# mLSTM cell and squared-ReLU FFN on one Trainium2 core: two more chunks attended in 64x64 quarters, and the first group's FFN2 placed ahead of the third group's FFN1

## The chip, the cores and the metric

The kernel runs on one core of one Trainium2 chip. The metric is device time in microseconds (us), start to end of one execution. PE is the engine for matrix products, DVE the vector engine, ACT the scalar engine, POOL GpSimd, SP the engine whose queue issues most transfers.

## The reference

Inputs are q, k, v and three gates for 4 batches, 8 heads, 768 steps, head width 40, all float32, and two FFN weights that arrive as float64. The first part is a recurrence over the steps, the second an FFN on its 3072 rows of 320:

```python
for t in range(S):
    m_new = np.maximum(f[:, :, t] + m, i[:, :, t])
    fs = np.exp(f[:, :, t] + m - m_new); is_ = np.exp(i[:, :, t] - m_new); m = m_new
    C = fs * C + is_ * outer(v[t], k[t]);  n = fs * n + is_ * k[t]
    y[:, :, t] = sigmoid(o[:, :, t]) * (C @ q[t]) / np.maximum(np.abs(n @ q[t]), 1.0)
h = np.maximum(x @ w_in, 0.0)          # x: y as rows; w_in 320 x 2048
out = h * h @ w_out                    # w_out 2048 x 320
```

## The kernel before

**Chunks.** The 768 steps of a batch are six chunks of 128 (`NB`), so there are 24, counted `s` = 0 to 23; all eight heads of a chunk are done together. A chunk needs: scores (k times q), weights W (exponential of a masked gate sum `A_bc`), `weighted` (their product P), the products of P with v, the carried state C, and the state after it. Chunk s = 5 closes batch 0 and makes no state. Two chunks are a group of FFN rows, `g` = 0 to 11.

**Two ways to attend.** Up to s = 5, `attend` uses full-height products: `hi` (state, L622), `dC` (new state, L634), `hp` (P and v, L645). `normalise` makes the rows x, and `turn_rows` transposes them on PE (L848, L850) with a copy on ACT (L853). From `X_SQ` = 6 on, `attend_begin` and `attend_end` use 64x64 quarters into `numT` (state L708, P and v L727, new state L738). Between the two halves stands a handshake: DVE reads one element of the first half and writes it to a spare place that the second half's operand covers (L700). The result comes out turned, so it goes through 32x32 blocks and memory: `store_num`, `load_num`, `normalise_turned`, `store_rows`, `load_rows`, `turn_squares`. `decays` (ACT) and `scale_q` (DVE, L672) prepare q times the decay. From `KQ_SQ` = 7 on, k and q are turned in the same way: `pair_up`, `load_squares`, `turn_kq`.

**The FFN.** `ffn1` of groups 0 and 1 is four plain parts each. From group 2 on, FFN1 is a seven-product scheme in two halves (`ffn1_open`, `ffn1_close`, with `sums_of_x` on the input and `sums_of_win` on the weights), each product X, Y, V, Z being blocks of four matmuls (L1041) and small rows (L1090). FFN2 of group 0 is plain (`ffn2`, L911: four parts, two row blocks by two halves of `w_out`); later groups use the same scheme (`ffn2_fast`, L965) with weight sums T0, T1, T2 and a changed `w_out` block (`sums_of_weights`), and input sums S1, S2, S4 (`sums`).

**The weights** come as 18 pieces. Each is fetched raw (SP), split into words on ACT (`words`), joined by three DVE instructions (L231, L235, L236) and one POOL addition (L240). `join` also issues the fetch of a later piece, whose buffer the join frees. `NEXT` and `LAST` say how many pieces are joined by which point.

**Order.** There is no planner: each engine carries out its instructions in the order in which the code issues them. A first loop, `u` = 0 to 7, does the FFN1 of groups 0 and 1 with chunks 2 to 5: even `u` makes scores of s = 2 + u // 2 and the next chunk's weights, odd `u` attends. A second loop runs over `parts`, with n = 0, 1, ... and four parts to a chunk (from s = 6): at n % 4 = 1 the chunk is attended, at 2 the next one's weights are made. `parts` begins with FFN1 of group 2 (kind 1) and then FFN2 of group 0 (kind 2).

## Time and profile before

| | us |
|---|---|
| median of 3 runs (lowest, highest) | 491.14 (490.63, 491.87) |
| the profiled execution: time, span | 491.22, 489.4 |
| PE busy, share of the span | 481.7, 98% |
| DVE, ACT, POOL busy | 341.8, 240.4, 215.3 |
| first loop from u = 4 to its end | 57.5 to 89.2 |
| FFN1 of group 2, FFN2 of group 0 | 91.0 to 109.0, 110.0 to 130.0 |
| FFN2 of group 1 begins | 130.8 |

The span is what the profile covers; the rest of the time lies around it. A row of a group gives busy time and the mean of one instruction; an fp32 matmul appears as two records. "Released by" names the instruction that ended an idle time.

### The profile page before, as it was taken

What the parts mean: (1) busy time and instruction counts of PE and PEld (TensorE: products, weight loads), DVE (VectorE), ACT (ScalarE), POOL (GpSimd) and SP (SyncE); (2) the same over time, 40 slices, a digit from 0 to 9 for tenths busy, and PEclk for the clock granted to TensorE, in tenths of its full rate; (3) what the DMA queues carried; (4) which work ended last, traced back from release to release, by engine and by line L of the source; (5) the groups of instructions that cost most, each with busy time, mean ns of one, the idle gap of its engine ahead of it and who ended that gap; (6) DMA issues with size and microseconds to landing.
All of it is one profiled execution on the core that took longest, in us unless ns stands there. A gap on an engine that the chain in (4) does not pass through costs nothing.

```text
span 489.4 us, 15237 instructions
## 1 busy us (share of the span) xinstructions
PE 481.7 (98%) x6169; PEld 449.0 (92%) x6169; DVE 341.8 (70%) x704; ACT 240.4 (49%) x531; POOL 215.3 (44%) x322
## 2 busy tenths in 40 slices
PE   9999999999999999999999999999999999999997
PEld 4886788897799999999999999999999999999996
DVE  7799767888946856957966956857856956635441
ACT  4676996764522650942742941742942640513300
POOL 6455533432679178078179078078174040020000
PEclk9999999999999999999999999999999999999999
DMA  9999997745878579758759778658665612200000
GB/s 185 227 243 227 304 230 183 151 84 140 171 130 199 120 138 225 134 107 212 135 99 219 140 117 208 134 109 213 123 106 129 149 51 82 55 28 2 3 27 29
DMA packets 191096, 68.08 MB, mean 139 GB/s; under 512 B 158833, under 2 KB 180241, under 8 KB 191025
## 3 DMA queue, kind: packets, MB, share of 16 engines
q1 hardware_dynamic: 185280, 57.50, 55.1%
q0 software_dynamic: 5600, 9.50, 8.1%
q8 instruction: 49, 0.80, 0.7%
q14 instruction: 23, 0.18, 0.1%
q10 hardware_dynamic: 144, 0.10, 0.1%
HBM read 54.77 MB, written 18.01 MB: 149 GB/s over the span
## 4 chain that ended last, share of the span: by engine, by line
PE 87%; ACT 5%; SPq 4%; DMA 3%; issue 1%; DVE 0%; ACTq 0%
PE h_ps L965 35%; PE h_ps L1041 26%; PE h_ps L1090 8%; PE h_ps L911 4%; PE h_ps L874 3%; PE numT L727 3%; PE numT L708 2%; DMA lent_t<-in_moe_w_in_dram 1%; PE numT L738 1%; SPq L210 1%; PE tp L575 1%; PE h_ps L575 1%; SPq L1151 1%; ACT g_c L511 1%; DMA raw<-in_moe_w_in_dram 1%; DMA og<-in_o_gate_dram 1%
## 5 line engine op out<-in xcount | busy, mean ns | idle before, releaser
L475 POOL TENSOR_SCALAR_AFFINE_SELECT A_bc<-A_bc 64x512 f32<-64x512 f32 x32 | 22.5, 704 | 80.4 <-ACT kq L492 57.9
L965 PE MATMUL h_ps<-T,S 128*128 128x160 f32 x352 | 51.7, 300 | 0.6 <-ACT g_c L1107 0.6
L1071 ACT COPY r_sb<-h_ps 128x512 f32<-128x512 f32 x18 | 10.5, 585 | 84.2 <-PE h_ps L1041 84.2
L965 PEld LDWEIGHTS h_ps<-T,S 128*128 128x128 f32 x352 | 48.9, 190 | 1.1 <-ACT g_c L1107 0.9
L965 PE MATMUL h_ps<-w_out,g 128*128 128x160 f32 x336 | 49.2, 303 | 0.0
L981 DVE TENSOR_TENSOR y_sb<-y_sb,h_ps 128x160 f32<-128x160 f32 x44 | 14.1, 320 | 47.7 <-PE h_ps L965 47.6
L965 PEld LDWEIGHTS h_ps<-w_out,g 128*128 128x128 f32 x336 | 46.1, 190 | 1.3 <-issue 0.5
L1041 PE MATMUL h_ps<-xT,w_in 128*128 128x128 f32 x320 | 42.8, 278 | 0.0
L1041 PE MATMUL h_ps<-lent_t,w_in 128*128 128x128 f32 x320 | 42.2, 275 | 0.0
L1041 PEld LDWEIGHTS h_ps<-xT,w_in 128*128 128x128 f32 x320 | 38.9, 192 | 1.4 <-issue 1.0
L1090 PE MATMUL h_ps<-xT,w_in 64*64 64x128 f32 x960 | 39.1, 272 | 0.0
L1041 PEld LDWEIGHTS h_ps<-lent_t,w_in 128*128 128x128 f32 x320 | 38.9, 192 | 0.2 <-issue 0.2
L1041 PE MATMUL h_ps<-lent_t 128*128 128x128 f32 x320 | 39.0, 275 | 0.0
L1041 PEld LDWEIGHTS h_ps<-lent_t 128*128 128x128 f32 x320 | 37.3, 192 | 0.0
L505 ACT ACTIVATE A_bc<-A_bc,b_R 128x64 f32<-128x64 f32 (+1 forms) x128 | 35.7, 361 | 1.8 <-POOL A_bc L475 1.4
L1090 PEld LDWEIGHTS h_ps<-xT,w_in 64*64 64x64 f32 x960 | 34.8, 133 | 1.3
L379 POOL DMA_DIRECT2D va<-in_v_dram x56 | 34.2, 619 | 1.8 <-DMA kq_rows<-in_q_dram 1.3
L758 DVE STREAM_TRANSPOSE tn<-numT 128x256 f32<-128x256 f32 x36 | 14.0, 428 | 28.5 <-PE numT L708 19.2
L874 PE MATMUL h_ps<-xT,w_in 128*128 128x256 f32 x128 | 30.1, 385 | 1.6 <-ACT xT L853 1.2
L874 PEld LDWEIGHTS h_ps<-xT,w_in 128*128 128x128 f32 x128 | 23.4, 190 | 6.1 <-POOL w_in L240 1.6
L1033 POOL TENSOR_TENSOR lent_t<-xT 128x128 f32<-128x128 f32 (+1 forms) x18 | 14.6, 833 | 32.7 <-DVE xT L840 32.7
L965 PE MATMUL h_ps<-w_out,g_c 128*128 128x160 f32 x192 | 28.0, 302 | 0.0
(218 smaller groups left out, 1150.0 us busy)
## 6 DMA issues: line engine op xcount, KB each, us to landing
A_bc<-a_slots SPq DMA_DIRECT2D x32, 256.0 KB, 4.4
num_rows<-tn SPq DMA_DIRECT2D x18, 256.0 KB, 2.3
kq<-num_rows SPq DMA_DIRECT2D x72, 64.0 KB, 2.1
raw<-in_moe_w_out_dram SPq DMA_DIRECT2D x7, 640.0 KB, 5.4
kqT<-kq_rows SPq DMA_DIRECT2D x34, 128.0 KB, 3.3
og<-in_o_gate_dram SPq DMA_DIRECT2D x24, 160.0 KB, 4.9
out_dram<-y_sb SPq DMA_DIRECT2D x24, 160.0 KB, 3.1
raw<-in_moe_w_in_dram SPq DMA_DIRECT2D x7, 512.0 KB, 6.9
```

The costliest lines, as they stand in the source:

```text
L379: eng.dma_start(dst[HALVES[n], PR * (1 - late_keys) : PR * (2 - late_keys)], src[HALVES[late_keys], PR * m : PR * (m + 1)],)
L475: nc.gpsimd.affine_select(part, part, compare_op=ALU.is_ge, fill=-1e30, base=0, pattern=[[0, PR], [0, 2], [1, DP]], channel_multiplier=-1,)
L505: nc.scalar.activation(A[0][:, x, to], A[0][:, x, to], AF.Exp, bias=b_R[:, b, c, own, x : x + 1],)
L727: nc.tensor.matmul(d["numT"][m][HALVES[e], i, t0:], lhsT=va_w[s % NKQ][keys, at * D1 : at * D1 + DP], rhs=rhs, start=(s % NB == 0 and i == ...
L758: nc.vector.transpose(to[:, 2 * m : 2 * m + 2], d["numT"][m].rearrange("p c t -> p (c t)"))
L874: nc.tensor.matmul(hs[i][:, n, :], lhsT=w_in[:, a, fb * P : (fb + 1) * P], rhs=xT[:, :, a, :], start=(n == 0 and a == 0), stop=False,)
L911: nc.tensor.matmul(o_ps, lhsT=st["g2", g][:, fb, j * P : (j + 1) * P], rhs=w_out[:, fb, :], start=(fb == 0), stop=(fb == NF - 1),)
L965: nc.tensor.matmul(to, lhsT=lhsT[:, p], rhs=rhs[:, p, :], start=(start and p == 0), stop=(p == NPAIR - 1), skip_group_check=True,)
L981: add = lambda to, a, b: nc.vector.tensor_tensor(to, a, b, op=ALU.add)
L1033: sub = lambda to, a, b: eng.tensor_tensor(to, a, b, op=ALU.subtract)
L1041: nc.tensor.matmul(to[:, n, :], lhsT=lhsT[:, 4 * q + n, :], rhs=rhs, start=(start and n == 0), stop=True, skip_group_check=True,)
L1090: nc.tensor.matmul(to[cols, n, :], lhsT=w_in2[rows, 4 * q + n, cols], rhs=rhs, start=(start and n == 0), stop=True, skip_group_check=True,)
```

## The change

Chunks s = 4 and 5 take the quarters: `X_SQ` goes from 6 to 4. Their masks are laid on W after the exponentials (`mask_W`), since the decays need the unmasked sums; in `u` = 2 the weights and decays of s = 4 are issued ahead of the weight words. They keep the old state's layout (`C_flat`), whose mask `bdm` is replaced by two copies of half height. In the second loop FFN2 of group 0 comes first (its row blocks taken in turn), then FFN1 of group 2, whose special beginning goes. The squares and gates of s = 7 are loaded at `u` = 6, `normalise_turned` of s = 4 and 5 stands at the end of `u` = 7 and in n = 0, `scores(7)` moves to n = 1. The loads of s = 8 and 9 go from SP to POOL and to n = 2 and 3, and their output gates to n = 0, 2 and 3. One piece is joined at n = 0 rather than at `u` = 7, the last at n = 1 rather than n = 4; all four weight sums stand at n = 3 and 4. The diff, without its mechanical parts:

```diff
...
     SQ = 32
-    KQ_SQ, X_SQ, ROT = 7, 6, 8
+    KQ_SQ, X_SQ, ROT = 7, 4, 8
...
         src = src[b, :, c * P : (c + 1) * P, :].rearrange("h p d -> p h d")
-        eng = nc.sync if s < 10 else nc.gpsimd
+        eng = nc.gpsimd
...
         src = src[b, :, c * P : (c + 1) * P, :].rearrange("h p d -> p h d")
-        eng = nc.sync if s < 10 else nc.gpsimd
+        eng = nc.gpsimd
...
+    def mask_W(s):
+        nc.gpsimd.affine_select(
+            st[s]["W"], st[s]["W"], compare_op=ALU.is_ge, fill=0.0, base=0, pattern=[[0, H], [1, P]],
+            channel_multiplier=-1,
+        )
...
         if s % NB > 0:
-            e = st[s]["eA"] = kq_b[2 + s % 2][:, 1].rearrange("p (j two) d -> p j (two d)", two=2)
+            home = kq_b[2 + s % 2 if s >= NB else s - X_SQ - 1]
+            e = st[s]["eA"] = home[:, 1].rearrange("p (j two) d -> p j (two d)", two=2)
...
                 )
-            if s < X_SQ:
+            if s < NB - 1:
...
-    C_old = []
+    C_old, C_flat = [], []
+    def num_tile():
+        return old.tile([P, 4 * P], F32, name="num", bufs=1)
...
             Cd = st[s]["Cd"] = old.tile([P, PR, 2, D1], F32, name="Cd", bufs=1)
+            if s >= X_SQ:
+                st[s]["Cd"] = Cd = Cd[:].rearrange("p j i d -> p (j i d)")[:, : PR * D1].rearrange("p (j d) -> p j d", d=D1)
+                for i, rows in enumerate(HALVES):
+                    nc.gpsimd.tensor_tensor(
+                        Cd[rows], C_old[(s - 1) % 2][rows, :, i, :],
+                        st[s]["dec"][rows, i::2].unsqueeze(2).to_broadcast([DP, PR, D1]), op=ALU.mult,
+                    )
+                return
             nc.gpsimd.tensor_tensor(
-                Cd[:].rearrange("p j i d -> p (j i) d"), C_old[(s - 1) % 2][:].rearrange("p j i d -> p (j i) d"),
+                Cd[:].rearrange("p j i d -> p (j i) d"), C_old[(s - 1) % 2].rearrange("p j i d -> p (j i) d"),
...
             Cn = C_old[s % 2]
-            if c == 0:
-                nc.vector.tensor_tensor(Cn[:], dC[:], bdm[:], op=ALU.mult)
+            for i in range(2 if c == 0 else 0):
+                nc.vector.tensor_copy(Cn[HALVES[i], :, i, :], dC[HALVES[i], :, i, :])
...
     LIVE = [slice(DP * i, DP * i + D) for i in range(2)]
+    def state(s):
+        return (C_b if s >= NB else C_flat)[s % 2]
...
         else:
-            end, spare = out[1][DP : DP + 1, P : P + 1], C_b[(s - 1) % 2][0:1, 4 * D1 : 4 * D1 + 1]
+            end, spare = out[1][DP : DP + 1, P : P + 1], state(s - 1)[0:1, 4 * D1 : 4 * D1 + 1]
...
         d = st[s]
-        C = C_b[(s - 1) % 2]
+        C = state(s - 1)
...
                 i, j = rows[m], 2 * m + e
+                at = (2 * j + i if s == X_SQ else j) * D1
                 nc.tensor.matmul(
-                    d["numT"][m][HALVES[e], i, :], lhsT=C[LIVE[i], j * D1 : j * D1 + DP], rhs=d["eA"][LIVE[i], j, :],
+                    d["numT"][m][HALVES[e], i, :], lhsT=C[LIVE[i], at : at + DP], rhs=d["eA"][LIVE[i], j, :],
...
             values_of_C(s, (1, 0))
-        tn = attn.tile([P, P // SQ, PR, SQ], F32, name="tn", bufs=1)
-        to = tn[:].rearrange("p m c r -> p c m r")
+        if s < NB:
+            tn = num_tile()[:].rearrange("p (m c r) -> p m c r", c=PR, r=SQ)
+        else:
+            tn = attn.tile([P, P // SQ, PR, SQ], F32, name="tn", bufs=1)[:]
+        to = tn.rearrange("p m c r -> p c m r")
...
         if c + 1 < NB:
-            Cn = C_b[s % 2][:, : PR * D1].rearrange("p (m x) -> p m x", m=2)
+            Cn = state(s)[:, : PR * D1].rearrange("p (m x) -> p m x", m=2)
...
     def load_num(s):
-        N = st[s]["N"] = kq_b[s % 2][:, 1].rearrange("p h d -> p (h d)")
+        N = st[s]["N"] = kq_b[s % 2 if s >= NB else s - X_SQ - 1][:, 1].rearrange("p h d -> p (h d)")
...
         if part == 0:
-            st["o_ps"] = ps_h.tile([P, W], F32, name="h_ps")[:, :DM]
-        o_ps = st["o_ps"]
+            st["o_ps", j] = ps_h.tile([P, W], F32, name="h_ps")[:, :DM]
+        o_ps = st["o_ps", j]
...
-    def ffn1_begin(g):
-        new_g2(g)
-        xT = st["xT", g]
-        begun = st["begun"] = [
-            (ps_h.tile([P, 4, P], F32, name="h_ps"), ffn.tile([P, 4, P], F32, name="r_sb", bufs=4)) for _ in range(2)
-        ]
-        for q, (X, m1) in enumerate(begun):
-            blocks(X, F11, xT[:, 0, 0, :], q, True)
-            nc.scalar.copy(m1[:], X[:])
-        for q, (X, m1) in enumerate(begun):
-            blocks(X, F12, xT[:, 0, 1, :], q, False)
     def ffn1_open(g, q):
-        if q == 0 and g > 2:
+        if q == 0:
...
         xT, xs = st["xT", g], st["xs"]
-        begun = st["begun"].pop(0) if g == 2 else None
-        X = begun[0] if begun else ps_h.tile([P, 4, P], F32, name="h_ps")
-        Y, V, Z = [ps_h.tile([P, 4, P], F32, name="h_ps") for _ in range(3)]
+        X, Y, V, Z = [ps_h.tile([P, 4, P], F32, name="h_ps") for _ in range(4)]
         st["f1"] = X, Y, V, Z
-        m1 = begun[1] if begun else ffn.tile([P, 4, P], F32, name="r_sb", bufs=4)
-        U2, U4 = [ffn.tile([P, 4, P], F32, name="r_sb", bufs=4) for _ in range(2)]
+        m1, U2, U4 = [ffn.tile([P, 4, P], F32, name="r_sb", bufs=4) for _ in range(3)]
         st["U"] = U2, U4
-        if not begun:
-            blocks(X, F11, xT[:, 0, 0, :], q, True)
-            nc.scalar.copy(m1[:], X[:])
+        blocks(X, F11, xT[:, 0, 0, :], q, True)
+        nc.scalar.copy(m1[:], X[:])
...
-    NEXT = (5, 8, 10, 11, 12, 13, 14, 16)
+    NEXT = (5, 8, 10, 11, 12, 13, 14, 15)
...
                     idle(3)
-                turn_rows(s - 1)
+                if s - 1 < X_SQ:
+                    turn_rows(s - 1)
...
             if u == 2:
+                weigh(4, masked=True, vw=False)
+                decays(4)
...
             if u == 2:
-                mask(s + 1)
                 rounding.join()
+                mask_W(4)
                 rounding.join()
-                weigh(s + 1, masked=True)
+                values(4)
...
                     relu_half()
-                weigh(s + 1, masked=(u == 0), vw=(u > 0))
+                weigh(s + 1, masked=(u != 6), vw=(u == 6))
+                if u == 4:
+                    mask_W(5)
                 square_half()
+                if u > 0:
+                    scale_q(s)
+                if u == 6:
+                    load_squares(7)
+                    load_A(7)
...
                 half_tanh(3)
-            load_A(s + 2)
+            if u < 7:
+                load_A(s + 2)
...
                     half_tanh(r)
-            attend(s)
+            if s < X_SQ:
+                attend(s)
+            else:
+                attend_begin(s)
+                attend_end(s)
...
                 values(s + 1)
-            normalise(s)
+            if s < X_SQ:
+                normalise(s)
+            else:
+                store_num(s)
...
                 rounding.join()
-            for r in {5: (8,), 7: (9,)}.get(u, ()):
-                load(r)
-            for r in {5: (7,), 7: (8,)}.get(u, ()):
-                pair_up(r)
             if u > 4:
-                load_o(2 * s)
-                load_o(2 * s + 1)
+                pair_up(s + 3)
+                load_num(s)
...
             square_half()
+            if u == 5:
+                decays(5)
+            if u == 7:
+                normalise_turned(4)
+                store_rows(4)
...
         nc.gpsimd.memset(t[:], 0.0)
-    parts = [(1, 2, i) for i in range(4)] + [(2, 0, i) for i in range(4)]
-    for g in range(1, NG):
+    parts = []
+    for g in range(NG):
...
             parts += [(1, g + 2, i) for i in range(4)]
-    LAST = (17, 17, 17, 17, 18)
-    assert LAST[-1] == len(pieces)
+    ROUNDED = (17, 18)
+    assert ROUNDED[-1] == len(pieces)
...
     for n, (which, g, i) in enumerate(parts):
-        s, at = 6 + n // 4, n % 4
-        if n == 5:
+        s, at = NB + n // 4, n % 4
+        if n == len(ROUNDED):
...
             do(mask, s + 1)
-            if n > 4 and not even and not fast:
+            if not even and not fast:
...
             do(decay_C, s + 1)
-            if s > X_SQ and not fast and not even:
+            if not fast and not even:
                 do(turn_squares, s - 1)
-            if even:
+            if even and s > NB:
...
             do(store_num, s)
+            if n == 1:
+                load_rows(5)
+                turn_squares(4)
...
                 do(load_A, s + 2)
-        if 5 <= n < 8:
-            sums_of_weights(n - 5)
-        if n == 6:
-            sums(1, slice(0, NPAIR), (1, 2))
+        if n == 1:
+            sums_of_win(2)
         if n == 8:
-            sums_of_weights(3)
...
             sums(g, slice(0, NPAIR), (3 + i,))
-        if n == 0:
-            ffn1_begin(g)
-            sums_of_x(g)
-            sums_of_win(2)
-        if at == 3 and s >= 8 and s % 2 == 0 and s // 2 - 1 < NG:
+        if at == 3 and even and s // 2 - 1 < NG:
...
                 do(turn_squares, s - 1)
-            if n > 4:
-                do(scale_q, s + 1)
+            do(scale_q, s + 1)
...
                 ffn1_close(g, i // 2, i == 1)
-                if at == 1 and g > 2:
+                if at == 1:
...
         elif g == 0:
-            ffn2(g, *divmod(i, 2))
+            ffn2(g, i % 2, i // 2)
...
             ffn1_square()
-            if n < 4:
-                do(turn_kq, s + 1)
-                do(scale_q, s + 1)
...
                 do(load_A, s + 2)
-            if s > 6:
+            if s > NB:
...
             do(load_rows, s)
-            if s == 6:
-                do(pair_up, s + 3)
-        if s == 7 and at == 2:
-            pair_up(s + 3)
+            if s == NB + 1:
+                pair_up(s + 3)
+        if n in (2, 3):
+            load(6 + n)
+            load_o(8 + n)
...
             do(pair_up, s + 3)
-            do(pair_up, s + 4)
-        if s == 7 and at == 3:
+            if s > NB:
+                do(pair_up, s + 4)
+        if s == NB + 1 and at == 3:
             load(s + 3)
-        if even and at == 3:
+        if even and at == 3 and s > NB:
             do(load, s + 4)
+        for x in {3: (0, 1), 4: (2, 3)}.get(n, ()):
+            sums_of_weights(x)
+        if n in (6, 7):
+            sums(1, slice(0, NPAIR), (n - 5,))
...
             ffn1_square()
-        if n < 5:
-            while rounding.done < LAST[n]:
+        if n < len(ROUNDED):
+            while rounding.done < ROUNDED[n]:
...
```

## The prediction

> **What bounds the kernel now.** I read the page's busy shares and slices first, then busy time by stage, then the waits, then the chain of waits. `s` counts chunks from 0, so "chunks 5 and 6" are s = 4 and 5. Busy shares, and two rows of the 40 slices:
>
> ```profile
> PE 481.7 (98%) x6169; PEld 449.0 (92%) x6169; DVE 341.8 (70%) x704; ACT 240.4 (49%) x531; POOL 215.3 (44%) x322
> PE   9999999999999999999999999999999999999997
> DVE  7799767888946856957966956857856956635441
> ```
>
> PE is busy from first slice to last; DVE is at eight or nine tenths around slices 8 to 11. Busy time in the two stages that the change touches (start:end, length, PE, PEld, DVE, ACT, POOL):
>
> ```profile
> 57.50:91.00 33.50, 32.34 (x237) 26.61 (x235) 23.37 (x38) 28.45 (x57) 13.15 (x9) 1.00 0.95 201
> 91.00:130.90 39.90, 39.62 (x515) 33.06 (x513) 33.85 (x66) 23.90 (x52) 16.69 (x25) 1.00 0.61 125
> ```
>
> PE lacks 1.2 us in the first and 0.3 in the second; DVE has only 6 us free of 39.9 in the second. The waits (who, for whom: total, count, longest):
>
> ```profile
> ACT mag L220 <- DMA raw<-in_moe_w_in_dram: 4.6, 2, 4.3
> PE h_ps L874 <- ACT xT L853: 1.2, 1, 1.2
> PE numT L738 <- DVE kq L700: 0.3, 1, 0.3
> ```
>
> The second is PE's idle time at 60.56: ACT came late with a copy because it stood 4.27 us (44.6 to 48.9) for a raw weight piece. The third is the handshake of a chunk in quarters: PE's second half waits for a one-element DVE instruction that reads the first half's end. From the chain of waits (start, length):
>
> ```profile
> 65.35 1.05 PE hi L622 x8
> 66.40 0.89 PE dC L634 x8
> 67.29 1.75 PE hp L645 x16
> ...
> 74.47 0.37 PE tp L848 x2
> 74.83 0.37 PE tp L850 x4
> ...
> 81.01 1.05 PE hi L622 x8
> 82.06 1.75 PE hp L645 x16
> ...
> 114.54 0.38 PE numT L708 x8
> 114.92 0.44 PE numT L727 x16
> 115.36 0.26 PE numT L738 x16
> 115.85 0.44 PE numT L738 x16
> 116.29 0.46 PE numT L727 x16
> 116.97 13.12 PE h_ps L911 x48
> ```
>
> From 60.56 to 485.90 the chain is nearly all PE, so any PE time saved or lost before 131 us moves the end one for one, if no other engine becomes late.
>
> **What the skill says.** "TensorE: Matmul & The Clock Gate", Part 3, The mechanism: matmuls on separate tiles of the array overlap. The trace agrees: s = 7 in quarters lasts 2.43 us (114.54 to 116.97), s = 4 in full tiles 3.70. The same page, Architectural detail: "ACT/DVE are strict FIFO", and, in What's actually happening, an idle window of about 3.4 us halves PE's clock. Here PE's granted clock stays in the top tenth in all slices; its longest wait is 1.2 us, so no run shows the drop. "SBUF — State Buffer", Who interferes with whom: a DVE instruction with two SBUF inputs contends with a GpSimd instruction that reads SBUF. This agrees in kind: the multiply at L672 took 1.23 us at 124.90, beside POOL's multiply at 124.27, and 0.69 at 107.09 with no POOL work.
>
> **Gains, on PE's path.**
> 1. `weigh(4)` and the new `decays(4)` go ahead of the weight words on ACT: 2.6 + 1.25 us inside ACT's 4.27 us wait. The words still start at 48.9, but the eight exponentials no longer follow them, so `xT` is copied about 1.3 us earlier. PE's wait goes: -1.16, and -0.24 where the product at 52.65 ran 3.79 us against 3.55. `mask_W` takes the mask's place on POOL; POOL was idle 1.62 us there.
> 2. s = 4 in quarters: 3.70 to 2.43, -1.27 (handshake included).
> 3. s = 5 has no state to make: 2.80 to 0.38 + 0.44 + 0.28 (handshake) + 0.33 + 0.4 = 1.8, -1.0.
> 4. No `turn_rows(4)` and `(5)`: 2 x 0.74, -1.47.
>
> Sum -5.2: `scores(6)` would end at 85.9, not 91.06.
>
> **At nothing.** The FFN work of group 2 and FFN2 of group 0 keep their PE counts. Three memsets (0.37 + 0.23 + 0.23) leave POOL ahead of 6.2 us and one (0.38) comes at 16.7, and chunk 0's state is two DVE copies (2 x 0.33) for one multiply (0.49); the next PE work that reads it, at 17.86, follows PE's own products without a wait. Chunks 4 and 5 on DVE: normalising in rows (5.0 + 3.6) against quarters (multiply 0.69, handshake 0.16, two transposes 0.78, rows 1.84, turn 0.53, each twice, and 0.35) is +0.1 in all. ACT drops two copies of 0.48 and a small exponential, and adds four of 0.62 and two of 0.47: covered, ACT has 5 us free before 91, but at s = 5's load of gates it runs 1 us later.
> SP: each new round trip issues a store (0.34), four reads (1.75), a store of rows (0.38) and four reads (1.85), 4.3 us, about what the loads of s = 8 and 9 took (0.42 + 1.28 + 2.57). `load_squares(7)` and `load_A(7)` go in ahead of them at u = 6 (3.41 and 0.41 to issue), 10 us before they are read. The two loads go to POOL after `values(7)`, 7 issues each, 0.79 + 1.24 + 2.45 = 4.5; queued behind them are `mask(8)` and the decayed state, wanted by ACT at 122: two loads end near 116, so they hide with 4 us to spare. Without that cover `weigh(8)` slips.
>
> **Losses: DVE's queue.** Group 2's FFN1 used to be PE's cover while DVE worked; now FFN2 of group 0 is. Each stall below is PE waiting for DVE, with times after the gain.
> a. Between `scores(6)` and the handshake of s = 6, DVE has `weighted` 1.2, `turn_kq(7)` 1.16, one piece's words 1.87, `normalise_turned(5)` 1.84, another piece 1.87, handshake 0.2: 8.1 us, to 94.0. PE has FFN2 4.5, the first half 0.7, `scores(7)` 0.88: 6.1 us, to 92.0. **Stall 2.0.** Behind the handshake wait the rest of s = 6 and all of PE.
> b. `weigh(7)` now stands on ACT behind the copy of FFN2's first output, so it begins when part n = 2 ends: copy 0.42, eight exponentials 2.33, `weighted(7)` 1.2, `normalise_turned(6)` 1.84, three of four input sums 0.9: 6.7. PE has one part 4.37 and four blocks 0.9: 5.3. **Stall 1.4** before the second product of group 2.
> c. Four weight sums (1.45 + 1.42 + 1.42 + 1.42) were spread over four parts; two now stand ahead of group 2's first two evacuating additions and two behind them: 7.2 us with two additions of 0.6 and the last input sum, to the handshake of s = 7. PE has three products 2.7, first half 1.0, rows 1.77: 5.5. **Stall 1.8.**
> d. From there to the second product of FFN2 of group 1 (before: 133.12) DVE waits 1.05 for the second half of s = 7, then transposes and state 1.0, waits 0.85 for a product, four additions 2.4, `turn_kq` 1.16, rows 0.48, two additions 1.2, `scale_q` 0.61, `normalise_turned(7)` 1.84, S1 1.2, four additions 2.4, S2 1.2: 15.4. PE has second half 1.05, ten blocks 9.13, rows 1.9, scores 0.7, product 2.28: 15.0. **Stall 0.5.**
>
> Sum +5.7; before's own gaps in that stretch (0.28 and short issue gaps) are not lost a second time: about -0.5. The stalls are nowhere in the trace of before, so both ends: below, none forms (DVE reaches these points 2 us earlier than I place it), 0; above, one in five of some thirty two-input DVE instructions is longer by 0.54, as L672 was, +3. I take the middle, the sum of uncontended rows.
>
> **Sum.** -5.2 + 5.7 - 0.5 = 0.0 on the profiled execution's 491.22 us (span 489.4, 1.8 around it), which stands 0.08 above the median of the runs shown: **491.1**. A difference of 0.3% (1.5 us) is about what can be told from no change.
>
> **Rivals.**
> - *No change: gain and stalls cancel.* As summed, 491.1; own range 489.7 to 492.6. For it: DVE's 85% in the second stage. Against: two sums near 5 us must agree. Chance 0.35.
> - *Faster: DVE keeps up.* If stalls a and c do not form (they rest on DVE's place in its queue within 2 us), 491.1 - 3.8 = 487.3; all gone, 485.4. For it: DVE's total work to group 1's sums grows only by some 3 us. Half the stalls gone gives 488.3. Chance 0.31.
> - *Slower: the reads of s = 5's rows land late.* DVE reaches `normalise_turned(5)` at 90.1. SP frees at 82.3 (it waits for the last raw weight's buffer), stores, issues four gathers (2.5) and the reads (1.75), landing 2.1 later, at 88.9: 1.2 us to spare. From there each microsecond late stops DVE, the handshake of s = 6 and PE alike. The queues are at 0.95 share just before 91; if both trips take the 4.9 us of an output-gate load, not 2.3 and 2.1, the end is 5.4 - 1.2 = 4.2 later, 495.3; half of it, or the contention above, 493 to 494. Chance 0.34.
> - *The change doesn't bring FFN2 forward.* The last `w_out` piece is on DVE until about 99.2 and on POOL (1.54) until 100.8; its columns are wanted near 102.4. 1.6 us late or more, PE just waits in FFN2: 492 to 494, counted under slower.
>
> **Range.** 487.5 to 494.3 leaves out the cases where nearly all stalls vanish or both trips are slow. Chances 0.31 faster, 0.35 same, 0.34 slower.
>
> **What would show it.** Right: no PE idle near 59 us; `scores(6)` ending near 86; PE idle 1.5 to 2.5 us ahead of the second half of s = 6 and of s = 7, released by the one-element DVE instruction; about 1.4 us ahead of group 2's second product, released by DVE's input sums; FFN2 of group 1 starting near 130.5. Wrong: PE idle released by a DMA or POOL (rivals three, four), or FFN2 of group 1 starting before 128.

## The result, and the profile after

| | before | changed kernel |
|---|---|---|
| median of the runs (lowest, highest) | 491.50 of 4 (490.63, 492.04) | 504.49 of 4 (502.65, 506.10) |
| profiled execution: time, span | 491.22, 489.4 | 506.10, 504.4 |
| `scores(6)` ends | 91.06 | 87.39 |
| FFN2 of group 1 begins | 130.84 | 141.77 |
| from there to the end of the span | 358.56 | 362.63 |

The changed kernel is slower: ratio 1.0265, 95% interval 1.0222 to 1.0308. Its profiled execution is the slowest of the four. Line numbers have moved: the handshake is L718, P and v L746, the new state L757, FFN2 of group 0 L933, the FFN1 blocks L1063, FFN2 of later groups L987.

Page of the changed kernel, busy shares and two rows of slices; slices 8 to 11 are now PE's worst, and its granted clock dips there and once later:

```profile
PE 483.6 (96%) x6229; PEld 449.7 (89%) x6229; DVE 340.0 (67%) x719; ACT 242.8 (48%) x534; POOL 225.5 (45%) x335
...
PE   8999999597899999999999999998999999999997
...
PEclk9999999889899999999999999999899999999999
```

and the clock row of the kernel before:

```profile
PEclk9999999999999999999999999999999999999999
```

Busy time by stage (start:end, length, PE, PEld, DVE, ACT, POOL, granted PE clock, DMA share, GB/s):

```profile
57.50:91.00 33.50, 31.62 (x310) 25.27 (x307) 22.46 (x44) 30.44 (x59) 14.30 (x11) 1.00 0.97 218
91.00:110.00 19.00, 13.43 (x128) 9.44 (x127) 10.58 (x25) 2.58 (x4) 6.53 (x7) 0.82 0.59 121
110.00:131.00 21.00, 16.04 (x209) 13.51 (x208) 12.70 (x26) 6.54 (x20) 13.50 (x18) 0.93 0.60 137
```

PE is idle for 10.5 of the 40 us after 91, and in that stretch its granted clock falls, which it did nowhere in the kernel before. DVE is not fuller: 23.3 us where it had 33.9. It waits, too. The waits of the changed kernel (total, count, longest):

```profile
PE numT L757 <- DVE kq L718: 8.1, 3, 5.6
PE h_ps L1063 <- ACT kq L496: 2.7, 1, 2.7
PE numT L727 <- issue: 1.6, 1, 1.6
PE h_ps L896 <- ACT xT L875: 1.0, 1, 1.0
DVE dm L812 <- DMA kq<-num_rows: 8.8, 6, 3.5
```

The first holds 5.57 us at the handshake of s = 6 and 2.27 at that of s = 7. The second is the wait before group 2's second product (2.69); ACT's instruction ended in the same quarter of a microsecond as DVE's input sums, and e2 and e4 below, where the same wait is put down to `lent_t`, show that the sums are what PE waits for:

```profile
119.41 2.02 PE L1063 MATMUL h_ps<-lent_t 128*128 128x128 f32 x16 [2.69 <-ACT kq L496]
...
127.42 0.44 PE L757 MATMUL numT<-vw,kq 64*64 64x41 f32 x16 [2.27 <-DVE kq L718]
```

Where the longest began, in the chain of waits (start, length):

```profile
93.19 2.05 DMA kq<-num_rows
...
97.50 0.41 DVE mag L227
...
99.32 0.17 DVE kq L718
...
99.53 0.67 PE numT L757 x16
...
101.09 10.45 PE h_ps L933 x32
```

and SP's issues (start, length):

```profile
82.66 1.36 SPq L206 DMA_DIRECT2D raw<-in_moe_w_out_dram  x2
84.07 0.46 SPq L795 DMA_DIRECT2D num_rows<-num  x1
...
91.75 1.87 SPq L800 DMA_DIRECT2D kq<-num_rows  x4
```

The store of s = 5's result goes out behind two raw weight pieces of 640 KB; 7.7 us later it has landed and SP can issue the reads. DVE stands 3.53 us for them, then normalises, joins a weight piece and only then does the handshake.

**Where the 15.0 us of span went.** Ahead of `scores(6)` 3.67 gained. From there to FFN2 of group 1, 54.38 us instead of 39.78: waits of 5.57, 2.69 and 2.27, and slow matmuls behind them. From the second half of s = 6 to the end of FFN2 of group 0 it is 16.14 us (99.53 to 115.67); in e2, with no wait there, 13.80. Behind the wait at s = 7, 4.53 us (127.42 to 131.95) against 2.94 in e2. So the clock cost 2.3 + 1.6 = 3.9. After FFN2 of group 1 begins, 4.07 more: a wait of 0.61 before its second product, one of 1.56 at 350.7 for which the trace names nothing, slow matmuls behind that (10.76 us of blocks for 9.13), and rests.

### The profile page after: what moved, and what is told of

It reads as the page before. It is cut to its first block, busy times and chain, and to the rows that moved or that the text cites. A ratio compares the mean times of both kernels' runs of the same rounds, so it can differ in the third digit from the quotient of the medians.

```text
span 504.4 us, 15397 instructions
## 1 busy us (share of the span) xinstructions
PE 483.6 (96%) x6229; PEld 449.7 (89%) x6229; DVE 340.0 (67%) x719; ACT 242.8 (48%) x534; POOL 225.5 (45%) x335
## 4 chain that ended last, share of the span: by engine, by line
PE 82%; ACT 5%; DMA 4%; SPq 4%; DVE 3%; issue 2%; POOL 0%; DVEq 0%; ACTq 0%; POOLq 0%
PE h_ps L987 34%; PE h_ps L1063 25%; PE h_ps L1096 7%; PE numT L746 3%; PE h_ps L933 3%; PE h_ps L896 3%; PE numT L727 2%; PE numT L757 2%; DMA raw<-in_moe_w_out_dram 1%; DMA lent_t<-in_moe_w_in_dram 1%; SPq L206 1%; PE h_ps L579 1%; SPq L1156 1%; PE tp L579 1%; DMA og<-in_o_gate_dram 1%
## 5 line engine op out<-in xcount | busy, mean ns | idle before, releaser
L478 POOL TENSOR_SCALAR_AFFINE_SELECT A_bc<-A_bc 64x512 f32<-64x512 f32 x32 | 24.3, 758 | 83.5 <-ACT kq L496 60.7
L1077 ACT COPY r_sb<-h_ps 128x512 f32<-128x512 f32 x20 | 11.7, 585 | 88.4 <-PE h_ps L1063 88.4
L987 PE MATMUL h_ps<-T,S 128*128 128x160 f32 x352 | 51.7, 300 | 0.6 <-ACT y_sb L1007 0.6
L987 PEld LDWEIGHTS h_ps<-T,S 128*128 128x128 f32 x352 | 48.9, 190 | 1.2 <-ACT y_sb L1007 0.8
L987 PE MATMUL h_ps<-w_out,g 128*128 128x160 f32 x336 | 49.3, 303 | 0.3 <-issue 0.3
L987 PEld LDWEIGHTS h_ps<-w_out,g 128*128 128x128 f32 x336 | 46.1, 190 | 1.7 <-issue 1.1
L1063 PE MATMUL h_ps<-xT,w_in 128*128 128x128 f32 x320 | 44.6, 283 | 0.0
L1063 PE MATMUL h_ps<-lent_t,w_in 128*128 128x128 f32 x320 | 43.7, 281 | 0.0
L1063 PEld LDWEIGHTS h_ps<-xT,w_in 128*128 128x128 f32 x320 | 40.1, 195 | 1.9 <-issue 1.6
L1063 PE MATMUL h_ps<-lent_t 128*128 128x128 f32 x320 | 39.1, 275 | 2.7 <-ACT kq L496 2.7
L1063 PEld LDWEIGHTS h_ps<-lent_t,w_in 128*128 128x128 f32 x320 | 40.5, 198 | 0.0
L375 POOL DMA_DIRECT2D va<-in_v_dram x64 | 39.2, 625 | 2.1 <-DMA kq_rows<-in_k_dram 1.5
L1063 PEld LDWEIGHTS h_ps<-lent_t 128*128 128x128 f32 x320 | 37.3, 192 | 2.8 <-ACT kq L496 2.8
L896 PEld LDWEIGHTS h_ps<-xT,w_in 128*128 128x128 f32 x128 | 23.4, 190 | 6.1 <-POOL w_in L236 1.8
L987 PE MATMUL h_ps<-w_out,g_c 128*128 128x160 f32 x192 | 28.0, 302 | 0.0
```

The costliest lines, as they stand in the source:

```text
L375: eng.dma_start(dst[HALVES[n], PR * (1 - late_keys) : PR * (2 - late_keys)], src[HALVES[late_keys], PR * m : PR * (m + 1)],)
L478: nc.gpsimd.affine_select(part, part, compare_op=ALU.is_ge, fill=-1e30, base=0, pattern=[[0, PR], [0, 2], [1, DP]], channel_multiplier=-1,)
L896: nc.tensor.matmul(hs[i][:, n, :], lhsT=w_in[:, a, fb * P : (fb + 1) * P], rhs=xT[:, :, a, :], start=(n == 0 and a == 0), stop=False,)
L987: nc.tensor.matmul(to, lhsT=lhsT[:, p], rhs=rhs[:, p, :], start=(start and p == 0), stop=(p == NPAIR - 1), skip_group_check=True,)
L1063: nc.tensor.matmul(to[:, n, :], lhsT=lhsT[:, 4 * q + n, :], rhs=rhs, start=(start and n == 0), stop=True, skip_group_check=True,)
```

## The experiments

All times are medians; a ratio is to the kernel before on the same chip, with its 95% interval. The marks and lines are those of one profiled execution each, which can lie off its median: the changed kernel's is the slowest of its four, e12's (493.11) the fastest of its six. Four marks (start of FFN2 of group 0; second product of FFN2 of group 1; first FFN1 product of group 4; from there to the end):

| kernel | FFN2 g0 | g1, second | FFN1 g4 | rest | median | ratio |
|---|---|---|---|---|---|---|
| before | 109.97 | 133.12 | 148.77 | 340.6 | 491.50 | 1 |
| changed | 87.72 | 144.81 | 160.97 | 343.4 | 504.49 | 1.0265 |
| e1 store first | 88.55 | 143.78 | 160.49 | 342.0 | 503.17 | 1.0225 (1.019 to 1.0259) |
| e2 handshake first | 89.98 | 143.69 | 161.02 | 340.8 | 501.14 | 1.0199 (1.0162 to 1.0236) |
| e3 PE kept busy | 86.93 | 140.18 | 155.90 | 340.2 | 498.06 | 1.0135 (1.011 to 1.0161) |
| e4 group 2's side | 90.23 | 141.85 | 157.57 | 340.6 | 498.71 | 1.0144 (1.0114 to 1.0173) |
| e5 order alone | 90.23 | 139.24 | 154.96 | 340.4 | 497.99 | 1.0121 (1.0092 to 1.015) |
| e6 four edits | 86.96 | 142.87 | 158.68 | 341.8 | 502.99 | 1.0221 (1.019 to 1.0252) |
| e7 requeued | 86.42 | 138.04 | 157.93 | 344.4 | 502.25 | 1.0187 (1.0124 to 1.0249) |
| e9 transfers too | 88.16 | 131.81 | 154.96 | 342.3 | 498.86 | 1.0136 (1.0103 to 1.0168) |
| e12 sums on POOL | 87.03 | 132.51 | 150.22 | 341.2 | 496.35 | 1.0102 (1.0074 to 1.0129) |

### e1: the store ahead of the raw pieces

```diff
+            if s >= X_SQ:
+                store_num(s)
+            if u == 7:
+                rounding.hold = False
+                rounding.fetch()
             if u != 3:
                 rounding.join()
...
-            else:
-                store_num(s)
```

`hold` keeps back the fetch of the join at u = 6, so that both raw pieces go out behind the store.

> One edit to the changed kernel: the store of s = 5's turned rows is issued ahead of the two raw weight fetches (640 KB each) that stood in front of it on SP; nothing else moves. Theory A (the transfers: the store and the four reads behind it were late because 1.3 MB of raw weights filled the DMA engines first): the store lands about 2.5 to 3 us after its issue at 82.7 instead of 7.7 us, DVE's wait of 3.53 us for kq<-num_rows before normalise_turned(5) shrinks to under 1, the PE wait at the handshake of s = 6 goes from 5.57 to about 2, the granted clock stays above 0.95 between 91 and 110, and the time is 497.5 to 500 (5 to 7 us below the changed kernel: 3.5 of the wait and 2 to 3 of slow clock behind it). Rival B (the DVE queue alone, or four gathers that are slow whatever stands before them): the handshake wait stays above 4.5 us and the time within 1.5 us of the changed kernel's 504.5.

SP, DVE and PE of e1 (start, length; in brackets the idle time before and who ended it):

```profile
82.67 0.34 SPq L796 DMA_DIRECT2D num_rows<-num  x1
...
93.73 0.65 DVE L813 TENSOR_SCALAR dm<-kq 128x8 f32<-128x8 f32 x1 [1.06 <-DMA kq<-num_rows]
...
98.18 0.66 PE L758 MATMUL numT<-vw,kq 64*64 64x41 f32 x16 [3.38 <-DVE kq L719]
...
99.67 15.08 PE L934 MATMUL h_ps<-w_out,g 128*128 128x320 f32 x48
```

The store landed after 2.2 us instead of 7.6, and DVE's wait fell from 3.53 to 1.06, so the raw pieces in front were most of the delay: theory A's mechanism stands. The four reads, now behind the raw pieces, took 4.2 us (median) instead of 2.0. The theory's time does not stand: PE still waited 3.38 where about 2 was expected, the clock still fell, FFN2 was as slow as before, and 1.3 us is all that the median moved, less than the intervals of the two ratios can tell apart.

### e2: the handshake ahead of normalise_turned(5)

```diff
         if n == 0:
...
-            normalise_turned(5)
-            store_rows(5)
...
             do(attend_begin, s)
+            if n == 1:
+                rounding.step(); rounding.step()
...
+                normalise_turned(5); store_rows(5)
                 load_rows(5)
```

> One edit to the changed kernel: normalise_turned(5) with its store of rows, and the second of the two weight pieces joined in n = 0, go behind the handshake of s = 6 on DVE; the transfers stay as they are. Theory A+ (PE waits because the handshake stands in DVE's queue behind work that waits for a transfer): PE's wait at the second half of s = 6 falls from 5.57 to under 1 us although normalise_turned(5) still waits for its reads until about 95, the granted clock stays at 0.97 or more from 91 to 110, and the time is 495 to 498. If PE instead stops in FFN2 for the last two weight pieces (they are then joined after 94 and wanted near 100), 1 to 3 us of that come back: 497 to 500. Rival B' (the stall only moves on, to the state of s = 6 or to the first sums of group 2, and the clock falls there): 502 or more.

PE and DVE of e2:

```profile
96.06 0.39 PE L757 MATMUL numT<-vw,kq 64*64 64x41 f32 x16
...
96.84 13.19 PE L933 MATMUL h_ps<-w_out,g 128*128 128x320 f32 x48
...
110.67 0.58 DVE L862 STREAM_TRANSPOSE xT<-xT 128x384 f32<-128x384 f32 x1 [3.99 <-DMA xT<-x_rows]
...
116.66 3.46 PE L1063 MATMUL h_ps<-lent_t 128*128 128x128 f32 x16 [5.75 <-DVE lent_t L1058]
```

The wait at s = 6 is gone and FFN2's three parts take 13.19, not 14.81. But PE then waits 5.75 for the input sums: the rows of s = 5 are stored at 105 and read back by 110.6, and all of DVE's work for s = 7 stands behind their turn. The wait moved, as rival B' had it, though 501.14 us lies between its 502 and theory A+'s 500.

### e3: PE kept busy during the wait

```diff
                 do(lambda s: scores(s, ("h", "h")), s + 1)
+            if n == 1:
+                idle(22)
```

> One edit to the changed kernel: 22 matmuls of zeros (128 x 512, bfloat16, to a spare tile) between scores(7) and the second half of s = 6, so that PE is busy during most of its wait there; DVE's wait and the time of the handshake stay as they are (99.3). Theory C (part of the loss is the clock that falls after the idle time): the granted clock stays at 0.97 or more from 91 to 110, the three parts of FFN2 behind it take 13.1 to 13.4 instead of 14.8 and the second half of s = 6 about 0.5 less, and the time is 501.5 to 502.8, some 2 to 3 us below the changed kernel. Rival (the clock fell for another reason, such as the load of the engines over a longer time): the clock is 0.82 to 0.9 there all the same and the time is 504 to 505.5.

PE of e3:

```profile
93.34 4.76 PE L1145 MATMUL idle<-zeros 128*128 128x512 bf16 x21 [0.16 <-issue]
...
98.75 0.44 PE L757 MATMUL numT<-vw,kq 64*64 64x41 f32 x16 [0.65 <-DVE kq L718]
...
99.58 13.19 PE L933 MATMUL h_ps<-w_out,g 128*128 128x320 f32 x48
...
116.36 2.76 PE L1063 MATMUL h_ps<-lent_t 128*128 128x128 f32 x16 [2.69 <-ACT kq L496]
...
124.37 0.44 PE L757 MATMUL numT<-vw,kq 64*64 64x41 f32 x16 [0.72 <-DVE kq L718]
```

The handshake comes as late as before, 11.8 us after FFN2 begins, and the matmuls behind it run at full clock: 13.86 us to the end of FFN2 instead of 16.14. That 2.3 us is shown to be the clock. The median fell by more, 6.4 us: in this execution the wait of 1.56 near 350 and the slow stretch behind it are absent too (rest 340.2, not 343.4), and so is PE's wait near 60. Whether by chance or by where the work lies in time, the runs don't tell. The same holds for the second product of group 2: behind a wait of 2.69 us in both, the two groups of matmuls that follow take 2.76 + 1.91 us here and 2.02 + 1.06 in the changed kernel. These slow matmuls in turn fill most of the wait at s = 7, 0.72 instead of 2.27, and full clock follows it.

### e4: group 2's side

```diff
+            if n == 2:
+                weigh(7, masked=True)
             ffn2(g, i % 2, i // 2)
...
-        for x in {3: (0, 1), 4: (2, 3)}.get(n, ()):
+        for x in {2: (0, 1, 2), 5: (3,)}.get(n, ()):
```

> Two edits to the changed kernel, both behind FFN2 of group 0: the exponentials of s = 7 are issued ahead of the copy of FFN2's first output on ACT, and three of the four weight sums are made at n = 2, where DVE is idle for 7.5 us, the fourth at n = 5. Theory D (PE waits for the two queues): the waits of 2.69 us (second product of group 2) and of 2.27 us (handshake of s = 7) go to under 0.5 each, the slow blocks after the second one (2.07 and 1.60 us instead of 1.06) go with it, the 5.57 us wait at s = 6 stays, and the time is 498 to 500. Rival (one of the two is limited by something else, such as the slowed clock at 110 to 131 or the read of s = 6's rows): a wait of over 1.5 us stays in 117 to 131 and the time is above 501.

PE of e4:

```profile
119.11 2.02 PE L1063 MATMUL h_ps<-lent_t 128*128 128x128 f32 x16 [0.53 <-DVE lent_t L1058]
...
124.65 0.39 PE L757 MATMUL numT<-vw,kq 64*64 64x41 f32 x16
```

The wait of 2.69 is 0.53, that of 2.27 is gone, blocks run at 1.16 and 1.06 behind it, and 498.71 is in the band of theory D: the two queues together were the cause of both; which edit removed which wait was not tried apart. Two shorter waits come later, 0.80 at 133.9 and 0.99 before the second product of FFN2 of group 1.

### e5: the order alone

`X_SQ` is 6 again, with full tiles and `turn_rows` for s = 4 and 5; the rest as changed. In it the query of s = 5 is overwritten by the squares of s = 7 before the state product reads it, so that chunk's values differ; PE's instructions and their order do not.

> One part of the change alone: FFN2 of group 0 ahead of FFN1 of group 2, with its weight sums, late piece and loads where the change has them, but s = 4 and 5 attended in full tiles with turn_rows as before (no quarters, no round trip through memory for them). Theory E (the order costs, through the DVE and ACT queues; the quarters only add the late reads): the wait at the handshake of s = 6 is under 1 us, since neither the wait for kq<-num_rows nor normalise_turned(5) stands before it; the waits before the second product of group 2 (2 to 3 us) and at the handshake of s = 7 (1.5 to 2.5) stay, with 1.5 to 3.4 us of slow clock behind them; the time is 496.5 to 500, that is 5 to 8 over the kernel before. Rival F (the order costs nothing by itself, the quarters' transfers are the whole loss): 490.5 to 493.

PE of e5:

```profile
97.85 0.44 PE L757 MATMUL numT<-vw,kq 64*64 64x41 f32 x16 [1.34 <-DVE kq L718]
...
115.43 3.42 PE L1063 MATMUL h_ps<-lent_t 128*128 128x128 f32 x16 [2.67 <-ACT kq L496]
...
123.44 0.44 PE L757 MATMUL numT<-vw,kq 64*64 64x41 f32 x16 [0.89 <-DVE kq L718]
```

That product takes 3.42 us, not 1.95. With no quarters and no round trip for s = 4 and 5 the time is 5.6 us over before, of the changed kernel's 13.0. Theory E holds in the main: the order costs by itself, and the reads came late only with the quarters' round trip. Two of its waits are not of the size expected: 1.34 at s = 6, where under 1 was, and 0.89 at s = 7, where 1.5 to 2.5 was; the slow product ahead of the latter fills part of it, as in e3. What the quarters win is 3.4 us of PE (1.16 and 0.72 in the attending parts and 1.47 in `turn_rows`, below).

### e6, e7, e9, e12: taking the waits away one after the other

e6 is e1, e2 and e4 together. e7 has e1's store and e4's exponentials, the sum 3 of `w_in` at n = 1, the input sums ahead of `weighted(7)` and `normalise_turned(6)`, and DVE's queue in another order:

```diff
-    WIN_SUMS = {5: 0, 6: 1, 7: 3}
+    WIN_SUMS = {5: 0, 6: 1}
...
             do(attend_begin, s)
+            if n == 1:
+                normalise_turned(5); store_rows(5); load_rows(5)
+                rounding.step(); rounding.step()
...
+            if n == 2:
+                sums_of_x(2)
...
+        for x in {3: (0,), 5: (1,), 8: (3, 2)}.get(n, ()):
```

e9 adds SP's and POOL's queues (`load_rows(6)` behind s = 7's store and reads, `load` of 8 and 9 at n = 3 and 6); e12 adds `sums_of_weights` 0 to 2 on POOL at n = 2 and 5, and the reads of s = 9's squares ahead of those rows.

> The edits of the three earlier runs together: the store ahead of the raw fetches, normalise_turned(5) behind the handshake of s = 6 and behind both weight pieces, the exponentials of s = 7 ahead of FFN2's first copy, the weight sums at n = 2 and n = 5. Theory A+D: the wait at the handshake of s = 6 is under 1 us and the granted clock from 91 to 110 at 0.97 or more. But normalise_turned(5), and so the reads of its rows, come late, and turn_squares(5) stands ahead of all of DVE's work for s = 7 and of the input sums, so PE still waits 3 to 6 us before the second product of group 2, with up to 1.7 us of half clock behind it; no wait at s = 7. Time 494 to 498. Rival (the exponentials of s = 7 were what made that wait): under 1 us there, time 489 to 492.

> The change with DVE's queue put in another order: the store of s = 5 ahead of the raw fetches; the last sum of w_in (1.22 us) from u = 7 to n = 1; the handshake of s = 6 ahead of normalise_turned(5), which keeps its place ahead of the last two weight pieces and has its rows stored and read at once; the exponentials of s = 7 ahead of FFN2's first copy; the input sums of group 2 ahead of weighted(7) and normalise_turned(6); the weight sums at n = 3, 5, 8 and 8. Theory (waits of PE for DVE's queue, and the clock behind each, are the whole loss): no PE wait above 0.7 us between 88 and 131, granted clock 0.97 or more there, FFN2 of group 1 begins 39.5 to 41 us after scores(6) ends (changed kernel: 54.4), and the time is 488 to 491.5, no slower than before by more than 0.3%. Rival (DVE has not the time: about 85% busy before, it is late somewhere else whatever its order): a new wait of 2 us or more, at s = 7 or in FFN2 of group 1, and 493 or more.

> The kernel of e7 with SP's and POOL's transfers put in another order as well: the rows of s = 6 are read back only after s = 7's store and four reads have been issued (in e7 SP stood 5.6 us waiting for those rows to be stored, and s = 7's store, ready at 115, was issued at 122.8), turn_squares(6) goes to n = 10, and the loads of s = 8 and 9 go to n = 3 and 6 instead of 2 and 3. Theory (the 8.4 us wait in FFN2 of group 1 in e7 is this queue of transfers, no want of DVE time): s = 7's store is issued before 118, DVE's wait of 7.3 us for kq<-num_rows at 124 goes to under 1.5, the wait in FFN2 of group 1 to under 1.5, and the time is 488 to 493, level with the kernel before or up to 0.6% from it. Rival (DVE's time is short): the wait stays above 4 us, 497 or more.

> The kernel of e9 with 4.9 us taken off DVE: the weight sums T0, T1 and T2 are made on POOL, at n = 2 and n = 5, where it has no work for s = 7 and 8 pending (about 3 us each there, by its 1.54 us for 640 words), and the reads of s = 9's squares go ahead of the rows of s = 6 on SP. Theory H (after the reorderings DVE's time itself is what holds PE: in e9 PE waits 1.1, 1.0 and 3.8 us in FFN2 of group 1 for DVE, and behind them the clock is halved for 3.4 us): the 3.8 us wait at s = 8's handshake goes to under 1 us and the other two to under 1 together, the second half of s = 8 runs near 136 instead of 141, and the time is 489 to 492.5, level with the kernel before. Rival I (the transfers hold it: DVE waited 2.1 us for kqT<-kq_rows ahead of that handshake): 1.5 us or more stay there and the time is 494 or more. Rival J (POOL's sums slow the DVE instructions beside them by more than they take off): as rival I, with two-input DVE instructions of 128 x 512 at 1.2 instead of 0.68 us between 106 and 125.

PE of e6:

```profile
118.56 3.61 PE L1064 MATMUL h_ps<-lent_t 128*128 128x128 f32 x16 [10.67 <-DVE lent_t L1059]
```

The wait before the second product is 10.67 us, where I expected 3 to 6: the weight sums, now ahead of the input sums, add 4.5 to the late rows. In e7 PE runs without a wait over 0.5 us from 88 to 121, then waits 1.07 for DVE, and FFN2 of group 1 begins at 127.2, 41 us after `scores(6)`, about as the theory had it. Its time does not come out, since then follows (SP, DVE, PE of e7):

```profile
122.82 0.53 SPq L796 DMA_DIRECT2D num_rows<-tn  x1
...
131.35 0.17 DVE L813 TENSOR_SCALAR dm<-kq 128x8 f32<-128x8 f32 x1 [7.34 <-DMA kq<-num_rows]
...
138.04 4.34 PE L988 MATMUL h_ps<-T,S 128*128 128x160 f32 x15 [8.37 <-ACT g_c L1124]
```

s = 7's result was ready at 115; its store went out at 122.8, because SP stood 5.6 us for the store of s = 6's rows, which took 6.1 us beside POOL's loads, against 2.1 in the changed kernel. The Trainium skill, "DMA: Bandwidth & Descriptors", Issuing engines are not separate DMA queues, says that transfers of SP and POOL interleave on the same engines; this trace agrees. In e9 that wait is 1.1 us, but three together (1.1, 1.0, 3.8) and a halved clock behind the last come in FFN2 of group 1 (PE of e9):

```profile
131.81 2.41 PE L988 MATMUL h_ps<-T,S 128*128 128x160 f32 x16 [1.14 <-ACT g_c L1124]
...
141.12 0.66 PE L758 MATMUL numT<-vw,kq 64*64 64x41 f32 x16 [3.76 <-DVE kq L719]
```

In e12 the 3.8 is 0.7 and the 1.0 is gone, but the 1.1 has grown to 3.33 (DVE and PE of e12):

```profile
125.70 0.17 DVE L813 TENSOR_SCALAR dm<-kq 128x8 f32<-128x8 f32 x1 [2.01 <-DMA kq<-num_rows]
...
131.08 1.22 DVE L983 TENSOR_TENSOR S<-S,g 128x1024 f32<-128x1024 f32 x1
...
132.51 2.41 PE L988 MATMUL h_ps<-T,S 128*128 128x160 f32 x16 [3.33 <-ACT g_c L1124]
```

S2, the sum at 131.08, is an operand of the product that waits. The last FFN1 product ends at 124.2; the rows, scores and the first product of FFN2 give PE 5 us. DVE has in that time `normalise_turned(7)` 1.9, S1 1.2, four additions 2.4, S2 1.2, 6.7 us, and starts when the reads of s = 7 land. Of the 3.33 us, 2.01 is DVE's wait for these reads. What is left, 1.3 by subtraction, and 1.14 in e9, where DVE did not wait for them, lies in the order itself: in the kernel before, FFN2 of group 0, some 17.7 us of PE that asks nothing of DVE, lay just there. Theory H's waits came out partly (3.8 to 0.7, not the other two together), and its time did not: 496.35. Two of the six executions of e12 kept full clock throughout (a mean of 1.000) and took 493.11 and 493.85; the other four, at 0.992 to 0.997, took 496.2 to 498.4. No version tried is faster than the kernel before; the best is 1.0102 (1.0074 to 1.0129).

### e8, e10: PE kept busy near 60 us

Five matmuls of zeros at u = 4, added to e7 and to e9.

> The kernel of e7 with five matmuls of zeros (about 1.1 us) between scores(4) and the FFN1 part at u = 4, where PE waits about 1.2 us for the copy of xT. Theory C (a wait of that length can send the clock to half for some 3.4 us, as in two of the four runs so far, where the 16 matmuls behind it took 5.41 us instead of 3.72): these 16 matmuls take 3.72 us and the time is 0.5 to 1.7 us below e7, with less spread. Rival (the halving there comes from something else): no difference beyond 0.5 us.

> The kernel of e9 with the five matmuls of zeros at u = 4 as in e8. Theory C (PE's wait of about 1.2 us for xT at u = 4 halves the clock in some executions): the spread of the times is smaller and the median 0 to 1.5 us below e9. Rival: no difference beyond 0.5 us.

500.49 (498.05 to 503.69) beside e7's 502.25 (498.94 to 504.68), 498.16 beside 498.86: not told apart. In e7's profiled execution the wait at u = 4 was not there to be filled.

### e11: the weight words first again at u = 2

```diff
             if u == 2:
+                rounding.words()
                 weigh(4, masked=True, vw=False)
                 decays(4)
-                rounding.words()
```

> One part of the change undone: at u = 2 the weight words go ahead of the exponentials and decays of s = 4 on ACT again, all else as in the changed kernel. Theory G (ACT waits for the second raw piece until about 52.5 whatever stands before it; the exponentials, once hidden in one wait, now hide in the wait before it, and the decays are new work): 3.9 us of exponentials and decays now stand between the first piece's words, done at 50.1, and the second's, so these begin at 54 instead of 52.5, and PE's wait for xT near 60 goes from 1.0 to about 2.5; the time is 1.5 us above the changed kernel, to 3.2 where the clock drops. Rival (my prediction's reading: the exponentials on ACT decide, and putting them first brings 1.3 us): the wait grows by 1.3 as well, but the second piece's words begin as soon as the exponentials end and a wait for the raw piece never shows, in either order.

ACT at the words of the second piece, in the changed kernel:

```profile
52.53 0.80 ACT L216 ACTIVATE mag<-raw 128x640 f32<-128x640 f32 x1 [2.39 <-DMA raw<-in_moe_w_out_dram]
```

and in e11:

```profile
53.93 0.78 ACT L216 ACTIVATE mag<-raw 128x640 f32<-128x640 f32 x1
```

In e11 the second piece has landed by the time the exponentials are done, and `xT` is copied at 62.15 instead of 60.02; FFN2 of group 0 begins 2.3 us later; 506.86, ratio 1.0315 (1.0254 to 1.0377). Theory G holds for ACT. PE's wait came in another place than I had said: 1.85 us for POOL's `w_in` at u = 3, ahead of the point where it would have waited for `xT`, and half clock behind it (a group of matmuls that takes 3.29 us in the changed kernel took 4.97). The reordering is worth about 2 us beside the other order (the intervals of the two ratios overlap), but it only pays for the decays that the quarters add.

## Why the prediction was wrong

It said 491.1 us, range 487.5 to 494.3, no change the likeliest; 504.49 was measured, above the range. The step that failed is the sum of losses: loss a was sized at 2.0 us and measured 5.57, because the store of s = 5's result was priced as if nothing stood in front of it, and what a wait does to the clock behind it, 3.9 us, was put at nothing. The gain fell short as well. Of the 15.0 us of span, 1.5 is missing gain, 5.3 the losses a to c beyond their sizes, 3.9 the clock and 3.6 the end, loss d taken off; 0.7 is rests. By its steps:

- **Gain 1 did not come (1.40 predicted; u = 4's FFN part began 0.05 later than before).** What failed in it: "the eight exponentials no longer follow" the words. ACT could not use the time: the next words wait for their own raw piece until 52.53. In the kernel before these words also began at 52.52; the exponentials had filled that second wait exactly, so it did not show. Where the piece landed sooner (words at 51.66 in e3) PE's wait was gone. PE and ACT of the kernel before, and PE of the changed one:

```profile
60.56 3.72 PE L874 MATMUL h_ps<-xT,w_in 128*128 128x256 f32 x16 [1.16 <-ACT xT L853]
52.52 0.77 ACT L220 ACTIVATE mag<-raw 128x640 f32<-128x640 f32 x1
60.61 3.72 PE L896 MATMUL h_ps<-xT,w_in 128*128 128x256 f32 x16 [1.01 <-ACT xT L875]
```

- **Gains 2 to 4 came**: the attending parts went from 3.59 to 2.43 and from 2.70 to 1.98, two `turn_rows` (1.47) away; -3.67 in all at `scores(6)`, with nothing from gain 1, against -5.2.
- **Loss a: 2.0 predicted, 5.57.** By subtraction DVE's queue gave the 2.0 (5.57 less DVE's 3.53 wait); the 3.53 is the rival *Slower: the reads of s = 5's rows land late*, mechanism and place as written, with 4.2 for both trips slow. I had written that SP stands until 82.3 for the last raw weight's buffer, and yet priced the store that follows at its usual 2.3 us instead of behind 1.3 MB.
- **Loss b: 1.4 predicted, 2.69**: my chain from the copy to the input sums left out POOL's `vw` (0.75), and PE's part behind the copy took 4.1, not 4.37. **Loss c: 1.8, 2.27**: one weight sum took 1.95. **Loss d: 0.5, 0.61**, near its size; the kernel before has no wait there (the product of the kernel before, then of the changed one):

```profile
133.12 2.34 PE L965 MATMUL h_ps<-T,S 128*128 128x160 f32 x16
144.81 2.41 PE L987 MATMUL h_ps<-T,S 128*128 128x160 f32 x16 [0.61 <-ACT y_sb L1007]
```

  That c came so near its size is in part luck: 0.72 and 0.89 stand in its place in e3 and e5, where the clock fell earlier.
- **The clock: not priced at all, 3.9 us there and about 1.6 near 350.** I quoted the skill's idle window and wrote that no run showed the drop; then I summed three waits of 1.4 to 2 us as if each cost only itself. e3 shows that the matmuls behind the wait at s = 6 are slower because of it; for the stretches behind s = 7 and near 350 it is inferred, not tried.
- **The end: 4.07 us** after FFN2 of group 1 begins, of which only loss d was in a step. 1.56 of it is a wait that the trace gives to nothing. It stands at the same instruction, or its neighbour, between 341 and 355 us, in the changed kernel (1.56) and in e1, e2, e6, e7, e9 and e11 (0.7 to 1.6), is 0.2 to 0.4 in e4 and e12, and absent in before, e3, e5, e8 and e10. Such nameless waits stand in two more places, none in before: in FFN2 of group 1 (0.28 in the changed kernel at 150.7, 0.83 to 0.88 in e1, e11 and e12) and in FFN1 of group 4 (0.7 to 1.67 in e6, e7, e9 and e10). What they are stays open.
- **The signs that I named.** No PE idle near 59: wrong, 1.01 us. `scores(6)` near 86: 87.39. FFN2 of group 1 near 130.5: 141.77. PE idle ahead of the second halves of s = 6 and s = 7 by the one-element instruction: right, though 5.57 at s = 6 is far over the 1.5 to 2.5. Before group 2's second product, by the input sums: right. "PE idle released by a DMA" as the sign of the slower rival: it came at one remove, DVE waiting for the DMA and PE for DVE. That FFN2 lacked its last weight piece did not happen.

Two sums of the prediction are out by 0.1, which changes nothing: the gains add up to 5.1, not 5.2, and loss c's terms give 1.7, not 1.8. My two sums near 5 us did not cancel: the gain was counted whole, the losses without what follows a wait. The rival for *faster*, that DVE keeps up, fails for a reason that the sum of DVE's work hides: DVE was less busy than before, and late because of what stood in front of it.

## What to carry to other kernels

A stage that asks nothing of the other engines is cover for what follows it; moving it forward uncovers the place that it left, and taking the waits away there one at a time shows the next one (s = 6, group 2's sums, s = 7's round trip, FFN2 of group 1), so price the whole stretch with every queue, DMA included, before counting a gain. A PE wait can cost more than itself: the shortest with half clock behind it was 1.16 us (e2), the most that followed was 2.9 us of extra matmul time (e7, 138.04 to 144.16: 6.12 us for what took 3.26 in the changed kernel). Before moving work into a wait, look what the engine waits for next: a second wait that is just filled does not show.

## What the runs showed of the hardware

- PE's clock halved, in some executions, behind a wait of 1.16 us: in e2 behind PE's wait at 60, the same 16 matmuls that took 3.72 us in before and in the changed kernel (waits 1.16 and 1.01) took 5.41, and in e4 behind 1.17 as well:

```profile
61.19 5.41 PE L896 MATMUL h_ps<-xT,w_in 128*128 128x256 f32 x16 [1.16 <-ACT xT L875]
```

  Two stretches of 2 us of e2 (third column from the end: granted clock):

```profile
60.00:62.00 2.00, 0.84 (x5) 0.70 (x4) 1.87 (x4) 2.00 (x7) 0.00 (x0) 0.91 0.89 105
62.00:64.00 2.00, 2.00 (x7) 1.53 (x6) 1.75 (x4) 2.00 (x7) 0.46 (x1) 0.50 1.34 178
```

  The Trainium skill, "TensorE: Matmul & The Clock Gate", What's actually happening, has PE at half clock after an idle window of about 3.4 us, and a free-running window of 3413 ns, from which it would follow that it matters where in it a wait falls. The length agrees: 1.69 us lost at half clock are 3.4 us of it, and the longer stretches are multiples. Behind the 5.57 us wait of the changed kernel the granted clock in stretches of 2 us from 96 on is 0.88, 0.50, 0.50, 0.50 and 0.92, together 6.8 us of half clock, of which some 4.8 fall behind the end of the wait; half of that is the 2.3 us lost, within 0.1. In e7 the half clock lasts 10.2 us. The coming and going between executions agrees too. That the array must idle for a whole window does not: a wait of 1.16 us was enough, though narrow transposes stand ahead of it and their share is not shown. A longer wait is no sure sign either: behind 3.33 us in e12 the clock stayed full.
- A 256 KB store issued right behind two raw pieces of 640 KB landed after 7.6 us, in e1, ahead of them, after 2.2. 192 KB beside POOL's loads took 6.1 us in e7, 2.1 in the changed kernel.
